# A fused attention and MLP kernel: work of the first batch moved between VectorE, ScalarE and GpSimd, score units reordered, last stores in two tiles

## Chip, cores, metric

One core of one Trainium2 chip (trn2). The metric is the device time of one execution in microseconds (us); less is better. Two kernels count as different when their executions differ by over 2%.

## The reference

Causal attention with a decay that is the cumulative sum of the positive part of `s`, in 8 batches of 8 heads, 576 positions and head size 64; then an MLP with exact gelu on the 4608 x 512 result.

```python
def _attn_ref(q, k, v, s):
    scores = scale * np.matmul(q, k.transpose(0, 1, 3, 2))
    cum = np.cumsum(np.maximum(s, 0.0), axis=-1)
    bias = -(cum[:, :, :, None] - cum[:, :, None, :])
    scores = np.where(causal, -1000000000.0, scores + np.minimum(bias, 0.0))
    attn = np.exp(scores - np.max(scores, axis=-1, keepdims=True))
    attn = attn / (np.sum(attn, axis=-1, keepdims=True) + 1e-09)
    return np.matmul(attn, v)

def _moe_ref(x, w_in, w_out):      # x: 4608 x 512, w_in: 512 x 2048, w_out: 2048 x 512
    h = x @ w_in
    return (0.5 * h * (1.0 + erf(h / sqrt(2)))) @ w_out
```

## The kernel before

The bias of key j is folded into v: row j of v is scaled by a weight `wb` and the weight itself is a 65th column, so one value matmul gives numerator and denominator. The parts that the change touches, with cuts marked:

```python
    def scale_v(b, st):
        n_st = 128 if st < ST - 1 else SL
        w = wb[:n_st, st, b * H : (b + 1) * H]
        nc.vector.tensor_tensor(
            vv[b % 2][:n_st, st, :, 0:D],
            raws[b, "v"][:n_st, st, :, :],
            w.unsqueeze(2).to_broadcast([n_st, H, D]),
            op=MULT,
        )

    def den_col(b):
        nc.vector.tensor_copy(vv[b % 2][:, :, :, D], wb[:, :, b * H : (b + 1) * H])
    # ...
    def av_item(b, g, it, later=False):      # value matmuls of four heads, one block of 128 queries
        # ... PE: lhsT=P[:, h, off:off+128], rhs=vv[b % 2][:, jt, 4*g+h, :]  (64 columns of v and the weight)
        nc.vector.reciprocal(rc[:n], o_ps[:n, :, D])
        nc.vector.tensor_tensor(x_of[b, it][...], o_ps[:n, :, 0:D], rc..., op=MULT)
    # ...
    # sc_first(g, u, halves, fill): score matmuls of group g, unit u, half by half, `fill` fillers, exp on ScalarE
    # mk_item: causal mask on P by VectorE;  to_xT: transposes on PE, copy to xT by VectorE
    # filler(n): n matmuls of zeros that keep PE busy
```

The eviction of the second layer, the order of the start, and the tail (the two copies of the tail are named in words here):

```python
            for sub in subs:
                o_sb = ost.tile([128, KO * 128], fp32, tag="osb", bufs=3, name="o_sb")
                if c == 0 and sub != 1:
                    nc.scalar.activation(o_sb, y_of[c, sub], func=AF.Copy)
                else:
                    nc.vector.tensor_copy(o_sb, y_of[c, sub])
                # ...
    load_v(0, nc.gpsimd, (0, 1))
    load_w(0, 0)
    load_w(0, 1)
    load_v(0, nc.gpsimd, (2, 3))
    load_w(0, 2)
    load_w(0, 3)
    # ... more loads, all issued by GpSimd, at most eight outstanding
    tr_qk(0, 0, 0)
    tr_qk(0, 1, 0)
    sc_first(0, 0)
    tr_qk(0, 0, 1)
    den_col(0)
    tr_qk(0, 1, 1)
    sc_first(0, 1, (0,))
    filler(2)
    sc_first(1, 0, (0,))
    mk_item(0, 0, 0)
    scale_v(0, 0)
    scale_v(0, 1)
    sc_first(1, 0, (1,))
    av_item(0, 0, 0)
    filler(1)
    mk_item(0, 1, 0, 0, 2)
    av_item(0, 0, 1)
    mk_item(0, 1, 0, 2, 4)
    sc_first(0, 1, (1,))
    filler(1)
    av_item(0, 1, 0)
    av_item(0, 1, 1)
    sc_first(1, 1, (0,), 0)
    to_xT(0, 0, True)
    filler(1)
    to_xT(0, 1, True)
    # ...
            o_sb = ost.tile([128, KO * 128], fp32, tag="osb", bufs=3, name="o_sb")
            for i, (copy, eng) in enumerate([(VectorE copy, nc.sync), (ScalarE copy, nc.scalar)]):
                cols = slice(i * 256, i * 256 + 256)
                copy(o_sb[:, cols], y[:, cols])
                eng.dma_start(out=out[r0 : r0 + 128, cols], in_=o_sb[:, cols])
```

## Time and profile before

| | before |
|---|---|
| median of 3 runs, us | 316.27 (315.94 to 316.29) |
| profiled run: time, span, us | 315.04, 313.3 |
| PE busy, granted clock | 96%, 0.998 |
| first score matmul, MLP start, us | 9.10, 18.52 |
| second layer of chunk 0, first layer of chunk 1 start, us | 35.81, 55.85 |
| last full eviction, last half copies (VectorE, ScalarE) start, us | 305.04, 308.96, 309.42 |

The profile is of one execution. PE is TensorE's matmuls (PEq its sequencer), DVE is VectorE, ACT is ScalarE, POOL is GpSimd and SP is SyncE; SBUF and PSUM are the on-chip memories, PSUM the one that matmuls write to. The granted clock is the share of TensorE's full clock that it was given. A landing is the end of a transfer. A timeline row has start, duration, engine, source line, operation, output and inputs, shape, the number of instructions merged in it, and in brackets the idle time of that engine just before with what ended it. Waits of a GpSimd load are for one of eight slots: load n waits for the landing of load n - 8.

### The profile page before, as it was taken

Reading aid. Unit: us, or ns where it says so; the run is one execution under the profiler, and the core shown is the slowest. Engines: PE = TensorE matmul, PEld = TensorE weight load, DVE = VectorE, ACT = ScalarE, POOL = GpSimd, SP = SyncE. Lnnn points to the kernel's source line nnn. Section 1 sums busy time; section 2 is a strip of 40 time slices with the busy share of each in tenths; the row PEclk is TensorE's granted clock in tenths of the full one; section 3 lists DMA queues with packets and bytes.
Section 4 is the critical chain, followed back from the end, with each engine's and each line's share of the span. In section 5 each row is a group of like instructions: output and inputs, shape, how many; then the busy total and the mean of one; then the engine's idle time right before and its main releaser. Section 6 shows DMA issues by size and latency. Waiting matters only on the chain. (4 is left out here: it accounts for less than half of the span.)

```text
span 313.3 us, 6063 instructions
## 1 busy us (share of the span) xinstructions
PE 301.7 (96%) x2478; PEld 155.6 (50%) x2520; DVE 200.0 (64%) x401; ACT 190.0 (61%) x256; POOL 53.0 (17%) x72
## 2 busy tenths in 40 slices
PE   8999999999999999999999999999999999999993
PEld 3487755544554455445454445444544555444441
DVE  7876657699769856975598559945895632250020
ACT  3686968877747673875586648756776666105400
POOL 8543440142002500070007000500000000000000
PEclk9999999999999999999999999999999999999999
DMA  7999999779521973188307961633101311010012
GB/s 135 219 229 211 225 216 284 149 144 209 143 74 27 210 168 96 25 172 199 103 18 173 175 137 32 145 74 96 52 17 42 103 52 25 33 68 36 1 68 75
DMA packets 30979, 36.46 MB, mean 116 GB/s; under 512 B 15648, under 2 KB 20000, under 8 KB 30944
## 3 DMA queue, kind: packets, MB, share of 16 engines
q0 software_dynamic: 11552, 23.07, 38.2%
q1 hardware_dynamic: 19248, 12.80, 14.2%
q8 instruction: 21, 0.34, 0.4%
q14 instruction: 14, 0.11, 0.1%
q10 hardware_dynamic: 144, 0.13, 0.1%
HBM read 36.85 MB, written 9.44 MB: 148 GB/s over the span
## 5 line engine op out<-in xcount | busy, mean ns | idle before, releaser
L483 PE MATMUL o_ps<-w_out_r,gT 128*128 128x512 bf16 x551 | 132.2, 379 | 2.4 <-issue 1.6
L467 PE MATMUL h_ps<-xT,w_in_r 128*128 128x512 bf16 (+1 forms) x625 | 131.4, 357 | 0.8
L472 ACT ACTIVATE gT<-h_ps 128x1024 bf16<-128x1024 f32 (+1 forms) x80 | 74.8, 939 | 63.6 <-PE h_ps L467 62.8
L467 PEld LDWEIGHTS <-w_in_r 128*128 128x128 bf16 x640 | 59.6, 98 | 53.8 <-issue 0.4
L483 PEld LDWEIGHTS <-gT 128*128 128x128 bf16 x576 | 51.9, 98 | 56.6 <-issue 3.1
L359 ACT ACTIVATE P<-sc_ps 128x1024 bf16<-128x1024 f32 x56 | 54.3, 1021 | 30.9 <-PE sc_ps L344 30.9
L122 POOL DMA_DIRECT2D raw_v<-in_v_dram x40 | 34.0, 864 | 128.0 <-ACT sq L213 115.9
L493 DVE COPY o_sb<-o_ps 128x512 f32<-128x512 f32 x32 | 22.1, 691 | 46.5 <-PE o_ps L483 46.5
L444 DVE RECIPROCAL rc<-av 128x4 f32<-128x4 f32 (+1 forms) x80 | 14.0, 175 | 39.4 <-PE av L435 39.4
L187 DVE STREAM_TRANSPOSE qkT<-raw_qk 128x576 f32<-128x576 f32 x32 | 37.4, 1243 | 0.7 <-DMA raw_qk<-in_k_dram 0.5
L435 PEld LDWEIGHTS <-P 128*128 128x128 bf16 x576 | 27.4, 98 | 17.2 <-DVE P L367 1.0
L445 DVE TENSOR_TENSOR x<-av,rc 128x256 bf16<-128x256 f32 (+1 forms) x80 | 33.8, 423 | 3.0
L205 DVE TENSOR_REDUCE amx<-raw_qk 128x2 f32<-128x2304 bf16 x14 | 35.1, 2534 | 0.0
L435 PE MATMUL av<-vv,P 128*128 128x65 bf16 x576 | 30.5, 193 | 1.0 <-DVE P L367 0.3
L221 DVE TENSOR_TENSOR vv<-raw_v,wb 128x512 bf16<-128x512 f32 (+1 forms) x40 | 26.0, 690 | 3.0 <-DMA raw_v<-in_v_dram 3.0
L367 DVE TENSOR_TENSOR P<-P,tri_bf 128x1024 bf16<-128x1024 bf16 (+1 forms) x33 | 22.1, 669 | 8.7 <-ACT P L359 8.7
L213 ACT ACTIVATE sq<-raw_v 128x512 bf16<-128x512 f32 (+1 forms) x40 | 24.9, 622 | 0.0
L344 PE MATMUL sc_ps<-qkT 32*128 32x256 bf16 (+2 forms) x560 | 18.2, 250 | 0.0
L344 PEld LDWEIGHTS <-qkT 32*128 32x128 bf16 x560 | 11.7, 92 | 12.4 <-issue 11.6
L498 ACT ACT_TABLE_LOAD x8 | 10.3, 1283 | 0.9 <-PEq L819 0.7
L419 PE MATMUL f_ps<-zero 128*128 128x512 bf16 x29 | 9.4, 448 | 1.2 <-DVE zero L150 1.2
L501 ACT ACT_TABLE_LOAD x8 | 10.3, 1283 | 0.1
(79 smaller groups left out, 89.9 us busy)
## 6 DMA issues: line engine op xcount, KB each, us to landing
out_dram<-o_sb SPq DMA_DIRECT2D x35, 256.0 KB, 2.2
raw_v<-in_v_dram POOLq DMA_DIRECT2D x32, 256.0 KB, 5.8
raw_qk<-in_q_dram POOLq DMA_DIRECT2D x7, 576.0 KB, 7.9
raw_qk<-in_k_dram POOLq DMA_DIRECT2D x7, 576.0 KB, 10.3
w_in_r<-in_moe_w_in_dram POOLq DMA_DIRECT2D x4, 512.0 KB, 11.8
w_out_r<-in_moe_w_out_dram POOLq DMA_DIRECT2D x4, 512.0 KB, 16.3
raw_v<-in_v_dram POOLq DMA_DIRECT2D x8, 128.0 KB, 6.6
raw_qk<-in_q_dram POOLq DMA_DIRECT2D x2, 288.0 KB, 5.5
```

The lines of the kernel that those rows point to most:

```text
L122: eng.dma_start(out=t[:n_st, st, :, :], in_=bass.AP(tensor=v.tensor, offset=v.offset + b * H * S * D + st * 128 * D, ap=[[D, n_st], [S * D ...
L187: nc.vector.transpose(qkT[b % 2][:, i, g, :S, :].rearrange("p s e -> p (s e)").bitcast(fp32) .rearrange("p (l j) -> p j l", j=LT), raws[b, ...
L205: nc.vector.tensor_reduce(amx[:, b * HG + g], raws[b, "qk"][:, :, g, :], axis=AX, op=ALU.max, apply_absolute_value=True,)
L213: nc.scalar.activation(sq[:n_st], raws[b, "v"][:n_st, st].rearrange("p h d -> p (h d)"), func=AF.Square, accum_out=sumv[:n_st, b, st : st ...
L221: nc.vector.tensor_tensor(vv[b % 2][:n_st, st, :, 0:D], raws[b, "v"][:n_st, st, :, :], w.unsqueeze(2).to_broadcast([n_st, H, D]), op=MULT,)
L344: nc.tensor.matmul(s_ps[h // 2][:, h % 2, off : off + n], lhsT=qk[r, 1, g, jt * 128 : jt * 128 + 128, e], rhs=qk[r, 0, g, i0 : i0 + n, e], ...
L359: nc.scalar.activation(P[:, 2 * h2 : 2 * h2 + 2, o : o + 512], s_ps[h2], func=AF.Exp, scale=scale)
L435: nc.tensor.matmul(o_ps[:, h, :], lhsT=P[:, h, off : off + 128], rhs=vv[b % 2][:, jt, 4 * g + h, :], start=(i == 0), stop=(i == len(BLK[it ...
L445: nc.vector.tensor_tensor(x_of[b, it][:n, g * 256 : g * 256 + 256].rearrange("p (h d) -> p h d", d=D), o_ps[:n, :, 0:D], rc[:n].unsqueeze( ...
L467: nc.tensor.matmul(h_ps[:, i, :], lhsT=w_in_r[:, ko, ft * 128 : (ft + 1) * 128], rhs=xT[:, ko, c * NB + n0 : c * NB + n1], start=(ko == 0) ...
L472: nc.scalar.activation(gT_of[c][:, f2 * 2 : f2 * 2 + 2, n0:n1], h_ps, func=AF.Gelu)
L483: nc.tensor.matmul(y_of[c, sub], lhsT=gT[:, ft, sub * 128 : (sub + 1) * 128], rhs=w_out_r[:, ft, :], start=(ft == 0), stop=(ft == FT - 1),)
```

## The change

The intent is to take VectorE off the path to the MLP: the denominators' column goes to ScalarE, the scaling of v's second block to GpSimd, the value matmuls of group 0 go ahead of a late score unit and four fillers go. The eviction of subtile 1 of chunk 0 goes to ScalarE. In the tail each half gets its own tile.

```diff
@@ -215,10 +215,10 @@
             accum_out=sumv[:n_st, b, st : st + 1],
         )
 
-    def scale_v(b, st):
+    def scale_v(b, st, eng=nc.vector):
         n_st = 128 if st < ST - 1 else SL
         w = wb[:n_st, st, b * H : (b + 1) * H]
-        nc.vector.tensor_tensor(
+        eng.tensor_tensor(
             vv[b % 2][:n_st, st, :, 0:D],
             raws[b, "v"][:n_st, st, :, :],
             w.unsqueeze(2).to_broadcast([n_st, H, D]),
@@ -487,7 +487,7 @@
         if f1 == FT and store:
             for sub in subs:
                 o_sb = ost.tile([128, KO * 128], fp32, tag="osb", bufs=3, name="o_sb")
-                if c == 0 and sub != 1:
+                if c == 0:
                     nc.scalar.activation(o_sb, y_of[c, sub], func=AF.Copy)
                 else:
                     nc.vector.tensor_copy(o_sb, y_of[c, sub])
@@ -514,6 +514,7 @@
     cum_sum()
     masks()
     weights()
+    nc.scalar.activation(vv[0][:, :, :, D], wb[:, :, 0:H], func=AF.Copy)
     filler(3)
     filler(3, raws[0, "qk"][:, 1, 0, :128])
     load_v(0, nc.gpsimd, (0, 1))
@@ -522,6 +523,7 @@
     load_v(0, nc.gpsimd, (2, 3))
     load_w(0, 2)
     load_w(0, 3)
+    scale_v(0, 1, nc.gpsimd)
     load_v(0, nc.gpsimd, (4,))
     load_qks(1)
     load_w(1, 0)
@@ -534,29 +536,25 @@
     tr_qk(0, 1, 0)
     sc_first(0, 0)
     tr_qk(0, 0, 1)
-    den_col(0)
     tr_qk(0, 1, 1)
     sc_first(0, 1, (0,))
-    filler(2)
+    filler(1)
     sc_first(1, 0, (0,))
     mk_item(0, 0, 0)
     scale_v(0, 0)
-    scale_v(0, 1)
-    sc_first(1, 0, (1,))
+    sc_first(1, 0, (1,), 0)
     av_item(0, 0, 0)
-    filler(1)
+    av_item(0, 0, 1)
     mk_item(0, 1, 0, 0, 2)
-    av_item(0, 0, 1)
+    sc_first(0, 1, (1,))
     mk_item(0, 1, 0, 2, 4)
-    sc_first(0, 1, (1,))
-    filler(1)
+    sc_first(1, 1, (0,), 0)
     av_item(0, 1, 0)
     av_item(0, 1, 1)
-    sc_first(1, 1, (0,), 0)
+    sc_first(1, 1, (1,), 0)
     to_xT(0, 0, True)
     filler(1)
     to_xT(0, 1, True)
-    sc_first(1, 1, (1,), 0)
     mk_item(0, 0, 1)
     scale_v(0, 2)
     mk_item(0, 1, 1)
@@ -794,14 +792,14 @@
     with tc.manual_schedule():
         for sub in range(LAST[1], 4):
             y = y_of[LAST[0], sub]
-            o_sb = ost.tile([128, KO * 128], fp32, tag="osb", bufs=3, name="o_sb")
             r0 = LAST[0] * NB + sub * 128
             for i, (copy, eng) in enumerate(
                 [(nc.vector.tensor_copy, nc.sync), (lambda o, a: nc.scalar.activation(o, a, func=AF.Copy), nc.scalar)]
             ):
                 cols = slice(i * 256, i * 256 + 256)
-                copy(o_sb[:, cols], y[:, cols])
-                eng.dma_start(out=out[r0 : r0 + 128, cols], in_=o_sb[:, cols])
+                o_sb = ost.tile([128, KO * 128], fp32, tag="osb", bufs=3, name="o_sb")[:, :256]
+                copy(o_sb, y[:, cols])
+                eng.dma_start(out=out[r0 : r0 + 128, cols], in_=o_sb)
 
 
 # ---- launch: one core; inputs and outputs as the reference has them ----
```

## The prediction

> **What bounds the kernel now.** I read the page from the top, then the start (first 60 us) and the last 18 us as timelines engine by engine, then the landing times of single transfers.
>
> The page's busy shares and slices:
>
> ```profile
> PE 301.7 (96%) x2478; PEld 155.6 (50%) x2520; DVE 200.0 (64%) x401; ACT 190.0 (61%) x256; POOL 53.0 (17%) x72
> PE   8999999999999999999999999999999999999993
> PEclk9999999999999999999999999999999999999999
> DMA  7999999779521973188307961633101311010012
> ```
>
> PE is busy from the first slice to the last at full clock; DMA is near full only in the first quarter. A gain must therefore remove PE waiting, or shorten the tail after the last matmul. The change touches three places: 9 to 20 us, 47 to 49 us, and the tail.
>
> The timelines of PE and DVE at the start (start, duration, engine, line, operation, idle time before and its releaser):
>
> ```profile
> 13.06 0.63 PE L389 MATMUL sc_ps<-qkT 32*128 32x256 bf16 x8
> 13.85 0.29 PE L435 MATMUL av<-vv,P 128*128 128x65 bf16 x4
> 14.19 0.40 PE L435 MATMUL av<-vv,P 128*128 128x65 bf16 x8
> 16.09 0.48 PE L435 MATMUL av<-vv,P 128*128 128x65 bf16 x10 [0.33 <-DVE P L367]
> 18.52 3.65 PE L467 MATMUL h_ps<-xT,w_in_r 128*128 128x256 bf16 x32
> ...
> 10.73 1.26 DVE L187 STREAM_TRANSPOSE qkT<-raw_qk 128x576 f32<-128x576 f32 x1
> 12.43 1.26 DVE L221 TENSOR_TENSOR vv<-raw_v,wb 128x512 bf16<-128x512 f32 x2
> 14.17 0.18 DVE L444 RECIPROCAL rc<-av 128x4 f32<-128x4 f32 x1 [0.48 <-PE av L435]
> 15.62 0.41 DVE L367 TENSOR_TENSOR P<-P,tri_bf 128x512 bf16<-128x512 bf16 x1
> 17.50 0.97 DVE L413 COPY xT<-xt_ps 128x512 bf16<-128x512 bf16 x2
> ```
>
> The MLP starts at 18.52 because the second xT copy ends at 18.47. Back from there the chain is DVE: reciprocal and scaling of each value item, the two half masks, the value matmuls at 16.09 that waited for the second mask. PE's fillers (0.21 us each) lie in its shadow.
>
> The second batch's stage, PE then DVE, and the tail's chain:
>
> ```profile
> 48.40 0.40 PE L435 MATMUL av<-vv,P 128*128 128x65 bf16 x8 [0.30 <-DVE xT L413]
> 47.33 0.68 DVE L493 COPY o_sb<-o_ps 128x512 f32<-128x512 f32 x1
> 47.93 0.75 DVE L413 COPY xT<-xt_ps 128x512 bf16<-128x512 bf16 x2
> 45.94 0.60 ACT L491 ACTIVATE o_sb<-o_ps 128x512 f32<-128x512 f32 x1 [0.66 <-PE o_ps L483]
> 46.95 1.94 ACT L359 ACTIVATE P<-sc_ps 128x1024 bf16<-128x1024 f32 x2 [0.42 <-PE sc_ps L344]
> ...
> 308.96 0.44 DVE o_sb L803
> 309.40 0.02 issue
> 309.42 0.38 ACT o_sb L800
> ```
>
> PE waited at 48.40 for an xT copy that stood behind the eviction at 47.33. In the tail ScalarE copies its half only after VectorE's, since both write one tile.
>
> **What the Trainium skill says.** "GPSIMD Engine Reference", Performance versus the Vector engine, puts a GpSimd tensor_tensor at about 2.6 cycles an element at 1.2 GHz (4497 ns for 2048 fp32). My estimate for 512 elements is 512 x 2.6 / 1.2 = 1.11 us plus some 0.1 us of dispatch, so 1.2 us against the 0.69 us on VectorE. The trace of before has no such instruction; its two affine selects of 128 elements start 0.25 us apart, 1.95 ns an element with one input, which fits. "SBUF — State Buffer", Who interferes with whom, says a VectorE instruction with two SBUF inputs contends with a GpSimd instruction that reads SBUF; no run yet shows it. VectorE's remaining scaling would hold the port until about 13.12. "DMA: Bandwidth & Descriptors", Issuing engines are not separate DMA queues, says that SP and ACT share the same 16 DMA engines; the tail agrees: two 128 KB stores, and the engines 90 to 99% busy at 310.8 to 311.1. "TensorE: Matmul & The Clock Gate", Part 1, says an idle window of about 3.4 us halves the clock. The trace grants full clock throughout with the fillers in; without four of them no gap I foresee exceeds 0.7 us.
>
> **The change part by part.**
>
> *Denominators on ScalarE.* Removes a 0.34 us copy at 10.35 from VectorE; ScalarE has 1.90 us idle before its first exponential at 9.76. But the transpose behind the removed copy started at 10.73, just when the last k block landed (issued 3.00, 7.7 us to landing, so 10.7). Worth 0.0.
>
> *One scaling on GpSimd.* It stands behind a weight load (10.99 to 11.74) and needs v's second block: issued at about 5.0, 7.9 us to landing, so 12.9. With the port free at 13.12 it starts at about 13.15, ends at 13.15 + 1.2 = 14.35, and PE sees it at T = 14.4. The next loads on this queue are issued some 2 us later (12.15 becomes 14.4), but eight transfers are outstanding and the DMA engines stay full, so landings should not move.
>
> *Reordering.* The first value item may start at 13.64, without its filler, and finish its VectorE part by 14.6. The second starts at T = 14.4, against 14.19 before. VectorE then does reciprocal (T + 0.43 = 14.83), scaling (+0.22), half mask (+0.34 = 15.39), half mask (+0.33 = 15.72, ends 16.13): before, that last mask ended at 16.03. So 0.1 us later. PE does the late score units meanwhile; the one between xT blocks is now ahead of them. From the mask on the chain is as before (16.03 to 18.52 is 2.49 us), so the MLP starts at 16.13 + 2.49 = 18.62, +0.1 us. Break-even is T = 14.3. The four fillers removed (4 x 0.21 = 0.85 us) are worth nothing directly. The last exponential would end near 18.4 instead of 19.63, but PE next needs a gelu only at 22.50, when the first is over by 21.6: worth 0.
>
> A gain here would also be cut short by the DMA. Two landings (issue times from the GpSimd timeline, then times to landing of those two issues, third quarter-blocks of weights):
>
> ```profile
> 10.99 0.75 POOL L147 DMA_DIRECT2D w_in_r<-in_moe_w_in_dram x1 [0.71 <-DMA raw_qk<-in_k_dram]
> DMA to landing us min/median/max: 13.9/13.9/13.9
> 25.17 1.51 POOL L147 DMA_DIRECT2D w_out_r<-in_moe_w_out_dram x2 [1.91 <-DMA w_in_r<-in_moe_w_in_dram]
> DMA to landing us min/median/max: 15.3/15.3/15.3
> ```
>
> The last block of the first weight lands at 10.99 + 13.9 = 24.9, and PE uses it at 24.95; the third of the second weight lands at 40.5 and is used at 40.59. So PE runs on the heels of its weights, and at most 0.1 us of an earlier MLP start survives. A later start is not recovered. I take +0.1 us for the stage.
>
> *Eviction of subtile 1 on ScalarE.* VectorE loses 0.68 us at 47.33, so the xT copy starts at 47.33 and ends at 47.75, and PE's value item goes at 47.94 instead of 48.40. ScalarE evicts at about 46.45 to 47.0, where it waited 0.42 us anyway. The next value item (49.50) needs a scaling that ended at 49.28 and would end at about 49.16, so only 49.50 - 49.22 = 0.28 us survives. PE is the bound from there to the end with no other wait for data, so it stays: -0.28 us.
>
> *Two tiles for the last halves.* ScalarE's copy moves from 309.42 to 308.96 and its store from 309.84 to about 309.38: 0.46 us. But data flow without a break from 310.25 to 311.19, 0.94 us for 262 KB (280 GB/s). Started together, at the 340 GB/s of the best tenths they take 0.77 us: end at 311.02, so -0.17 us instead of -0.46.
>
> Sum: +0.1 - 0.28 - 0.17 = -0.35 us, and 316.27 - 0.35 = 315.9 us.
>
> **The rivals.** (1) GpSimd is fast or starts early (T at 14.0): the chain gains 0.3 us, but the weights' landing lets only 0.1 us through: about 315.7. (2) GpSimd becomes the bound: its first elementwise instruction of this kind may carry a start-up cost, or the port is lost to VectorE. Each 0.5 us beyond T = 14.4 goes straight into the time; 316.4 to 317. For it: spans on this engine are the ones I know least; against: the queue is otherwise only issuing. (3) PE cools down for lack of fillers: half clock for some 3 us costs 1.5 us or more, about 317.5. Against: the gaps stay short and PE was dense before. (4) The weights land later because loads are issued 2 us later: against it, only transfers behind the fourth w_in block move, and the DMA is full; it would cost up to 0.5 us. (5) The tail gains its full 0.46 us because two queues overlap better: 315.6.
>
> **Range and chances.** Centre 315.9. The gain side is capped near 0.1 + 0.46 + 0.46 = 1.0 us (315.2); the loss side is rival 2 or 4, some 0.6 us (316.6). Times of before spread by 0.35 us, which the range covers too: 315.2 to 316.6. Two per cent is 6.3 us, more than any part can move: within 2% 0.98, faster 0.01, slower 0.01.
>
> **What would show it.** Right: no den copy on VectorE at 10.35 and the transpose still at 10.7; a GpSimd multiply of about 1.2 us from about 13.15; PE's second value item at about 14.4 waiting for GpSimd; MLP start at 18.5 to 18.8; PE's wait of 0.30 us for the xT copy gone; both tail copies at the same time, but last data only 0.1 to 0.3 us earlier. Wrong: a GpSimd span over 1.7 us or an MLP start beyond 19; a granted clock below 9 tenths in the first slices; PE waiting for w_in or w_out near 25 or 40 us; a total that moves by more than 1 us.

## The result

| | before | changed |
|---|---|---|
| median of 6 runs, us | 315.86 (315.35 to 316.29) | 315.62 (315.31 to 316.13) |
| ratio | | 0.9993, 95% interval 0.9979 to 1.0007 |
| profiled run, us | 315.04 | 315.94 |

The ratio is the mean time of one kernel's runs over that of the other's of the same rounds, so it is not quite the ratio of the medians. 315.62 lies in the predicted range. The gain is smaller than the spread of the runs, so single times say little here. I compare stages inside the traces, each counted from its own beginning.

The start of the changed kernel: PE, VectorE, ScalarE and GpSimd timelines.

```profile
10.23 0.63 PE L389 MATMUL sc_ps<-qkT 32*128 32x256 bf16 x8 [0.47 <-DVE qkT L187]
14.64 0.33 PE L435 MATMUL av<-vv,P 128*128 128x65 bf16 x5
15.21 0.37 PE L435 MATMUL av<-vv,P 128*128 128x65 bf16 x7 [0.24 <-POOL vv L221]
19.46 3.65 PE L467 MATMUL h_ps<-xT,w_in_r 128*128 128x256 bf16 x32 [0.52 <-DVE xT L413]
...
11.88 1.26 DVE L187 STREAM_TRANSPOSE qkT<-raw_qk 128x576 f32<-128x576 f32 x1 [0.27 <-DMA raw_qk<-in_k_dram]
13.58 0.67 DVE L221 TENSOR_TENSOR vv<-raw_v,wb 128x512 bf16<-128x512 f32 x1
14.98 0.18 DVE L444 RECIPROCAL rc<-av 128x4 f32<-128x4 f32 x1 [0.73 <-PE av L435]
...
8.53 0.38 ACT L517 ACTIVATE vv<-wb 128x40 bf16<-128x40 bf16 x1
14.05 1.10 POOL L221 TENSOR_TENSOR vv<-raw_v,wb 128x512 bf16<-128x512 f32 x1 [1.17 <-DMA raw_v<-in_v_dram]
```

Everything stands about 1.1 us later than before because the loads came later in this execution: the fourth transpose starts at 11.88 against 10.73, on its landing both times. That differs from execution to execution (the table of all traces below): the block was issued at 3.00 us before and 3.01 us here, and landed 7.7 and 8.8 us later. In all traces this took 7.2 to 8.8 us with a scaling on GpSimd and 7.0 to 8.0 us without, so a part of it may be the change's own; that is not shown. From the first score to the MLP it is 19.46 - 10.23 = 9.23 us against 18.52 - 9.10 = 9.42, a gain of 0.19 us where I had forecast a loss of 0.1. PE waited 0.24 us for GpSimd, and VectorE stood idle 0.73 us where it used to do the second scaling.

The second batch's stage and the tail of the changed kernel (timelines, then the chain that ended last: start, duration, engine):

```profile
48.65 0.39 PE L410 MATMUL xt_ps<-ident_bf,x 128*128 128x128 bf16 x4
48.88 0.41 PE L435 MATMUL av<-vv,P 128*128 128x65 bf16 x8
48.27 0.42 DVE L413 COPY xT<-xt_ps 128x512 bf16<-128x512 bf16 x1
46.87 1.09 ACT L491 ACTIVATE o_sb<-o_ps 128x512 f32<-128x512 f32 x2 [0.65 <-PE o_ps L483]
...
309.48 0.44 DVE o_sb L801
309.91 0.02 issue
309.94 0.38 ACT o_sb L797
```

PE's value item now follows the transposes without a wait, and from the second layer to the second chunk it is 56.48 - 36.74 = 19.74 us against 20.04. In the tail nothing changed: ScalarE's copy still starts 0.46 us after VectorE's, when that is done.

### The profile page after: what moved, and what is told of

It is laid out like the page before. It is cut to its first block, busy times and chain, and to the rows that moved or that the text cites. A ratio compares the mean times of both kernels' runs of the same rounds, so it can differ in the third digit from the quotient of the medians.

```text
span 314.2 us, 6059 instructions
## 1 busy us (share of the span) xinstructions
PE 302.0 (96%) x2475; PEld 155.5 (49%) x2516; DVE 199.0 (63%) x398; ACT 191.0 (61%) x258; POOL 54.5 (17%) x73
## 3 DMA queue, kind: packets, MB, share of 16 engines
q1 hardware_dynamic: 19248, 12.80, 14.4%
## 5 line engine op out<-in xcount | busy, mean ns | idle before, releaser
L493 DVE COPY o_sb<-o_ps 128x512 f32<-128x512 f32 x31 | 21.4, 691 | 46.5 <-PE o_ps L483 46.5
```

## The experiments

Twelve runs were made, of nine new kernels and, once more, the changed one. The stages of all traces, in us:

| run | first score | first score to MLP | first layer | second layer, to chunk 1 | last full eviction to last copy | span |
|---|---|---|---|---|---|---|
| before | 9.10 | 9.42 | 17.29 | 20.04 | 3.92 | 313.3 |
| changed | 10.23 | 9.23 | 17.28 | 19.74 | 3.93 | 314.2 |
| s_vec | 9.42 | 9.03 | 18.04 | 19.75 | 3.88 | 313.7 |
| s_twice | 9.01 | 12.10 | 18.06 | 19.73 | 4.18 | 316.4 |
| s_den | 9.87 | 9.20 | 18.66 | 19.73 | 4.02 | 315.3 |
| s_fill | 9.43 | 9.67 | 17.29 | 19.72 | 5.11 | 315.2 |
| t_banks | 9.88 | 9.21 | 17.41 | 19.73 | 5.97 | 316.7 |
| t_banks_one | 9.17 | 9.13 | 17.66 | 19.73 | 5.94 | 316.3 |
| e_only | 9.00 | 9.43 | 17.66 | 19.94 | 5.19 | 315.1 |
| w_early | 8.68 | 8.98 | 18.12 | 19.79 | 3.76 | 313.0 |
| after5 | 10.08 | 9.21 | 17.29 | 19.72 | 3.90 | 313.9 |
| vec5 | 8.73 | 9.09 | 18.37 | 19.73 | 3.77 | 313.3 |
| e_only3 | 9.54 | 9.42 | 17.28 | 19.72 | 4.16 | 314.6 |
| w_early2 | 9.12 | 8.99 | 17.29 | 20.63 | 4.00 | 313.6 |

### s_vec: the second scaling back on VectorE, in the new order

```diff
-    scale_v(0, 1, nc.gpsimd)
...
     scale_v(0, 0)
+    scale_v(0, 1)
```

> The changed kernel with the second scaling of v put back on VectorE, right after the first, everything else as changed. Measure: from the start of the fourth transpose of q and k (it starts when the last k block has landed, so the run's own loading speed drops out) to the first MLP matmul; 7.79 us in the profile of before (10.73 to 18.52), 7.58 us in that of the changed kernel (11.88 to 19.46). Theory: the gain of 0.21 us comes from the new order alone. VectorE stood idle 0.73 us before the first reciprocal, and a scaling of 0.69 us (0.6 us from start to start) fits there; its result would be ready some 0.3 us before GpSimd's. So 7.45 to 7.6 us. Rival: GpSimd's taking over the scaling is what pays; then VectorE's chain gets 0.6 us longer and this run shows 8.0 to 8.2 us.

It was 18.45 - 11.01 = 7.44 us from the fourth transpose to the MLP, a hair under the theory's range and far from the rival's. VectorE's and PE's timelines:

```profile
12.71 1.41 DVE L221 TENSOR_TENSOR vv<-raw_v,wb 128x512 bf16<-128x512 f32 x2
14.10 0.18 DVE L444 RECIPROCAL rc<-av 128x4 f32<-128x4 f32 x1
18.45 3.65 PE L467 MATMUL h_ps<-xT,w_in_r 128*128 128x256 bf16 x32 [0.52 <-DVE xT L413]
22.89 1.05 PE L467 MATMUL h_ps<-xT,w_in_r 128*128 128x256 bf16 x8 [0.31 <-DMA w_in_r<-in_moe_w_in_dram]
```

Both scalings fit before the first reciprocal, which no longer waits. So the gain is there without GpSimd, which takes 0.14 to 0.2 us of it back. It need not be the order's alone: this kernel also has the four fillers fewer, and s_fill below shows that they count. The old order without these fillers was not run. The last row shows the second finding: PE, early, waits for the first weight, and the first layer takes 18.04 us in place of 17.28.

### s_twice: GpSimd scales twice

```diff
     scale_v(0, 1, nc.gpsimd)
+    scale_v(0, 1, nc.gpsimd)
```

> The changed kernel with GpSimd doing its scaling twice (same result, the second over the first). Theory: the scaling on GpSimd lies on the chain to the MLP, since PE waited for it by 0.24 us and VectorE's chain follows; so the doubled 1.10 us goes straight into the measure: 7.58 + 1.0 to 1.1 = 8.6 to 8.7 us. Rival: it lies beside VectorE's and ScalarE's work with slack; then less than 0.5 us shows (under 8.1 us).

It was 21.11 - 10.43 = 10.68 us, 3.1 us more and not 1.05. GpSimd's row, PE's wait for it, and what the stretches were granted (columns: stretch, length, then busy time of PE, its weight loads, VectorE, ScalarE and GpSimd, each with its number of instructions, PE's granted clock, DMA share, GB/s):

```profile
12.80 2.17 POOL L221 TENSOR_TENSOR vv<-raw_v,wb 128x512 bf16<-128x512 f32 x2 [1.35 <-DMA raw_v<-in_v_dram]
15.02 0.37 PE L435 MATMUL av<-vv,P 128*128 128x65 bf16 x7 [1.38 <-POOL vv L221]
...
13.30:15.00 1.70, 0.34 (x7) 0.24 (x6) 0.60 (x2) 1.18 (x2) 1.62 (x3) 1.00 1.24 205
15.00:17.00 2.00, 1.51 (x27) 1.26 (x29) 1.27 (x4) 1.01 (x1) 2.00 (x3) 0.73 1.21 271
17.00:19.00 2.00, 2.00 (x34) 1.65 (x28) 1.10 (x4) 1.04 (x2) 0.86 (x2) 0.50 1.12 215
21.00:23.00 2.00, 1.89 (x11) 1.35 (x11) 2.00 (x6) 0.61 (x2) 0.70 (x2) 0.57 1.25 218
```

The wait grew by 1.38 - 0.24 = 1.14 us, which is the second scaling: GpSimd's result is on the path. Most of the rest, some 2 us, goes with the clock: after that wait PE was granted half of it from about 16 to 22 us, and from its second value item to the MLP it took 21.11 - 15.02 = 6.09 us against 19.46 - 15.21 = 4.25. The first layer began at this clock too. That is my rival of the cooling, met here and not in the changed kernel, whose wait was short. It was seen in this one execution; a wait of 1.10 us in s_den left the clock at 1.00.

### s_den: the denominators' column back on VectorE

```diff
-    nc.scalar.activation(vv[0][:, :, :, D], wb[:, :, 0:H], func=AF.Copy)
...
     tr_qk(0, 0, 1)
+    den_col(0)
     tr_qk(0, 1, 1)
```

> The changed kernel with the denominators' column back on VectorE, between the third and the fourth transpose. Theory: the fourth transpose waits for the landing of the last k block anyway, so the 0.34 us copy costs nothing: the measure stays at 7.58 us (7.5 to 7.65), and first transpose of the block to MLP likewise unless the block lands early. Rival: the copy delays the fourth transpose; then the transpose follows the copy without a wait for a transfer and the third-transpose-to-MLP time (9.11 us in the changed kernel, 10.35 to 19.46) grows by 0.3 us.

```profile
11.09 0.34 DVE L229 COPY vv<-wb 128x40 bf16<-128x40 bf16 x1
11.48 1.25 DVE L187 STREAM_TRANSPOSE qkT<-raw_qk 128x576 f32<-128x576 f32 x1
11.74 0.75 POOL L147 DMA_DIRECT2D w_in_r<-in_moe_w_in_dram x1 [0.73 <-DMA raw_qk<-in_k_dram]
24.32 1.05 PE L467 MATMUL h_ps<-xT,w_in_r 128*128 128x256 bf16 x8 [1.10 <-DMA w_in_r<-in_moe_w_in_dram]
```

From the fourth transpose to the MLP 19.07 - 11.48 = 7.59 us, and 9.20 us from the first score (9.23 with the column on ScalarE): the copy costs nothing. The transpose starts when the k block has landed: GpSimd's load, which waits for the same landing, follows 0.26 us later here as in before (10.73 and 10.99) and as in the changed kernel, which has no copy there (11.88 and 12.14). The third transpose to the MLP was 9.08 us (9.11), so the rival falls. In this run the weights were later still, and PE waited 1.10 us for them.

### s_fill: the four fillers put back

```diff
     sc_first(0, 1, (0,))
-    filler(1)
+    filler(2)
...
-    sc_first(1, 0, (1,), 0)
+    sc_first(1, 0, (1,))
     av_item(0, 0, 0)
+    filler(1)
     av_item(0, 0, 1)
...
     mk_item(0, 1, 0, 2, 4)
+    filler(1)
     sc_first(1, 1, (0,), 0)
```

> The changed kernel with its four removed fillers put back (one behind the first late score unit, one in the second of them, one between the two value items, one ahead of the next score unit). My prediction called them worth nothing directly. Theory: they lie partly in the shadow of VectorE's chain; at most the one ahead of the first value item delays a reciprocal, so 7.6 to 7.85 us. Rival 1: PE is the bound here and all four count, 4 x 0.21 = 0.85 us: 8.4 us. Rival 2: without them PE cools; then this run shows a higher granted clock at the start than the changed kernel, whose slices all show 9 tenths or more.

The measure that I had named reads 19.10 - 10.21 = 8.89 us, above theory and rival, and does not serve: in this run the k block landed early and VectorE then stood idle 0.61 us for ScalarE's exponential, so the chain did not hang on the fourth transpose. From the first score it is 9.67 us against 9.23: 0.44 us more, half of what all four fillers take (0.85 us), between theory and rival, and 0.25 us more than before: with these fillers kept, the changed start gains nothing. The granted clock was the same, so no cooling without them. One row besides was not foreseen. GpSimd and VectorE:

```profile
12.58 1.09 POOL L221 TENSOR_TENSOR vv<-raw_v,wb 128x512 bf16<-128x512 f32 x1 [1.36 <-DMA raw_v<-in_v_dram]
12.69 1.53 DVE L221 TENSOR_TENSOR vv<-raw_v,wb 128x512 bf16<-128x512 f32 x1
```

Here GpSimd's scaling started first, and VectorE's own took 1.53 us in place of 0.67, ending 0.55 us after GpSimd's end. It ended at 14.22 and the first value matmul ran at 14.27. By PE's own pace it would have come at about 14.17 (the filler before it at 13.95, and from a filler to a value matmul 0.22 us from start to start, 14.39 to 14.61 in this trace). So my estimate is that the blocked scaling has about 0.1 us of the 0.44 and the fillers the rest.

### t_banks and t_banks_one: the last subtile's sums in two banks of PSUM

The core of the edit, and with one output tile again in the second kernel:

```diff
+        if (c, subs[0]) == LAST:
+            for i in range(2):
+                y = yps.tile([128, 256], fp32, tag="mlp", bufs=2, name="o_ps")
+                for ft in range(FT):   # 256 columns of w_out each
+                    nc.tensor.matmul(y, lhsT=gT[...], rhs=w_out_r[:, ft, i * 256 : i * 256 + 256], ...)
...
-                copy(o_sb, y[:, cols])
+                copy(o_sb, y[i])
```

> The changed kernel with the last subtile's sums in two banks of PSUM, 256 columns each (16 + 16 matmuls of 256 columns in place of 16 of 512), so that VectorE and ScalarE each read a bank of their own; the two output tiles stay. In the changed kernel ScalarE's copy still waited for VectorE's (309.48 then 309.94), as before (308.96 then 309.42), so the two tiles took away no wait. Theory: what ScalarE waits for is the shared PSUM bank. Then both copies start within 0.05 us here, ScalarE's store is issued some 0.4 us sooner after VectorE's copy starts, and the last data of the stores end 0.1 to 0.25 us sooner, measured from the start of VectorE's copy (2.2 us in the profile of before). Rival: ScalarE comes late out of the branch for another reason; then it still starts 0.46 us behind.

> As the run with two banks, but with one output tile for both halves, as in the kernel before. Theory: the tile in SBUF never made the wait (the halves are disjoint columns), so both copies start within 0.05 us here too. Rival: the tile makes a wait of its own; then ScalarE starts 0.4 to 0.46 us behind VectorE even with two banks, and it took both changes.

The tail of the run with two banks and two tiles, then with two banks and one tile:

```profile
311.29 0.38 ACT L815 ACTIVATE o_sb<-o_ps 128x256 f32<-128x256 f32 x1 [15.30 <-PEq L676]
311.29 0.42 DVE L819 COPY o_sb<-o_ps 128x256 f32<-128x256 f32 x1 [5.28 <-PEq L676]
```

```profile
310.88 0.38 ACT L816 ACTIVATE o_sb<-o_ps 128x256 f32<-128x256 f32 x1 [15.29 <-PEq L676]
310.88 0.42 DVE L819 COPY o_sb<-o_ps 128x256 f32<-128x256 f32 x1 [5.26 <-PEq L676]
```

Both copies start at the same instant, with two tiles and with one. What made ScalarE wait lay in PSUM; the tile in SBUF had no part in it. The edit gives each half a bank and also a PSUM tile of its own; two tiles in one bank were not run, so bank and PSUM tile are not told apart. The Trainium skill, "PSUM — Partial Sum Buffer", section "PSUM bank collisions raise a hardware error", says that two engines may not read one bank of the same partitions at once and that software has to order them. The traces agree: 0.46 us of order with one bank, none with two.

The bulk of the stores' data ended 2.1 us after VectorE's copy began (2.2 before, 2.3 in the changed kernel), about what I had worked out. Yet the stores landed 3.1 and 3.3 us after their issue, in both runs, against 1.9 and 1.8 before (1.8 to 2.4 in all twelve other traces), and the execution ended 5.4 us after the copy began (4.3 before, 4.7 changed). And the copies themselves began 5.97 and 5.94 us after the last full eviction in place of 3.93, released by PE's sequencer at the branch. So in these two executions the copies start about 2 us later: 318.53 and 318.03 us in the profiled runs. These 5.97 us are not the branch alone, since the last subtile's matmuls lie in them: from their end, as the profile models it, to the copies it is 0.51 us before (308.45 to 308.96) and 2.51 us in t_banks (308.78 to 311.29). Why the branch is later was not tested, and the two banks need not be the reason. One thing goes with it: the four traces with over 5 us in that column of the table (s_fill, t_banks, t_banks_one, e_only) are the four whose queue q8 of instruction transfers shows 22 packets; the ten others show 21.

### e_only and e_only3: the kernel before with the one eviction on ScalarE

```diff
-                if c == 0 and sub != 1:
+                if c == 0:
```

> The kernel before with nothing but the eviction of subtile 1 of the first chunk moved to ScalarE. Measure: from the first matmul of the first chunk's second layer to the first matmul of the second chunk; 20.04 us before, 19.72 to 19.75 us in the changed kernel and in the four runs so far. Theory: this part alone makes those 0.3 us: 19.70 to 19.78 us, with the wait of PE for the xT copy gone; the start (first score to MLP) stays at 9.4 us. Rival: the shift of the start makes the difference; then 20.0 us here.

The first run read 19.94 us, between theory and rival, because PE waited for the second weight in it:

```profile
41.36 1.89 PE L483 MATMUL o_ps<-w_out_r,gT 128*128 128x512 bf16 x8 [0.41 <-DMA w_out_r<-in_moe_w_out_dram]
48.43 0.41 PE L435 MATMUL av<-vv,P 128*128 128x65 bf16 x8
...
310.39 0.42 DVE L803 COPY o_sb<-o_ps 128x256 f32<-128x256 f32 x1 [4.50 <-PEq L666]
```

> The kernel before with the one eviction on ScalarE, again, three rounds. In its first run the stage gained (19.94 against 20.04 us, though with a wait of 0.4 us for w_out in it), but the last copy came 1.2 us later after the branch than in before, released by PE's sequencer, with a third instruction fetch in the last 12 us where before has two; so had the run with the fillers put back. Theory: that late branch belongs to the program as laid out (same in every execution); then this kernel is 0.8 to 1.0 us slower than before in all rounds and its trace shows it again. Rival: it is chance; then it is 0.2 to 0.4 us faster than before and the trace most likely shows 3.9 us from the last full eviction to the last copy. The stage without a wait for w_out is to show 19.70 to 19.78 us.

The same kernel again, with no such wait:

```profile
48.15 0.39 PE L410 MATMUL xt_ps<-ident_bf,x 128*128 128x128 bf16 x4
48.37 0.41 PE L435 MATMUL av<-vv,P 128*128 128x65 bf16 x8
...
309.72 0.42 DVE L803 COPY o_sb<-o_ps 128x256 f32<-128x256 f32 x1 [3.47 <-PEq L666]
```

The stage took 19.72 us, with the start at 9.42 us: this part alone makes the 0.3 us. The late branch of the first run (5.19 us from the last full eviction to the last copy) was 4.16 us in the second, so the size of it is not fixed by the program; it varies from execution to execution. Its four times were 315.42 to 316.64 us, ratio 0.999 (0.996 to 1.0019): "always slower by 0.8 us" falls, and the gain is too small to be timed.

### w_early and w_early2: the first weight loaded ahead of v's later blocks (wrong results on purpose)

```diff
-    load_v(0, nc.gpsimd, (2, 3))
     load_w(0, 2)
     load_w(0, 3)
-    scale_v(0, 1, nc.gpsimd)
+    load_v(0, nc.gpsimd, (2, 3))
     load_v(0, nc.gpsimd, (4,))
...  (in scale_v, blocks 2 and 3 of batch 0 read raw blocks 0 and 1)
     scale_v(0, 0)
+    scale_v(0, 1)
```

> Wrong results on purpose: the changed kernel with both scalings on VectorE, whose third and fourth blocks of v are taken from the first two, so that their loads can go behind the four blocks of the first weight; these then have 512 KB less ahead of them (some 2.5 us at 205 GB/s). The kernel with both scalings on VectorE reached the MLP 0.2 us sooner than the changed one (9.03 against 9.23 us from the first score), but then PE waited 0.3 us and more for the weight and the first layer took 18.04 us instead of 17.28. Theory: the weights' landing eats the gain of the start; with the weights early the first layer takes 17.25 to 17.35 us with no wait for the weight, and the start stays at 9.0 to 9.1 us. Rival: the new order makes the first layer slower by itself; then it takes 17.7 us or more here too.

The first layer took 18.12 us, against the theory, but with no wait for the weight: what it waited for was the fifth block of v (1.0 us), whose load I had moved back. So in the second kernel `load_v(0, nc.gpsimd, (4,))` stands ahead of `load_v(0, nc.gpsimd, (2, 3))`:

> Wrong results on purpose, as the run with early weights, with the fifth block of v ahead of the third and fourth: in the first such run no wait for w_in was left, but PE waited 1.0 us for the fifth block's scaling (0.2 us otherwise), because its load had been put last; the first layer took 18.12 us. Theory: with that load early too the first layer takes 17.25 to 17.4 us, no wait for w_in, start 8.95 to 9.1 us, so the whole gain of the start arrives at the second layer. Rival: the new order slows the first layer by itself; 17.7 us or more.

The first layer took 17.29 us with the start at 8.99: the order does not slow it, the weight's landing does. PE's waits in that trace up to 58 us (who waited for what, us, times, longest):

```profile
PE o_ps L483 <- DMA w_out_r<-in_moe_w_out_dram: 1.1, 1, 1.1
PE h_ps L467 <- DVE xT L413: 0.5, 1, 0.5
```

So the gain reached the second layer at 35.40 us, and was lost there to the second weight (20.63 us in place of 19.73). Only in part because PE came sooner: this block of the weight landed at 24.92 + 16.4 = 41.3 us, against 40.5 in before. The second chunk began at 56.03 us, no sooner than in runs with a slow start (55.85 before).

### after5 and vec5: the changed kernel and the version without GpSimd's scaling, five rounds

> The changed kernel again, five rounds, for a trace of its own and beside the same rounds of the kernel before. From the parts measured so far (start -0.2, eviction -0.3, tail 0) 0.2 to 0.6 us under before, so a ratio of 0.998 to 0.9995. Theory on the weights: wherever the start got ahead of the loads, PE waits for w_in between 22 and 26 us, so the gain of the start is lost in some executions. Start 9.2 to 9.25 us from the first score, second layer to second chunk 19.72 to 19.75 us, ScalarE's last copy 0.46 us behind VectorE's.

> The version without GpSimd's scaling (both on VectorE, order and eviction as changed), five rounds: the candidate that should beat both. Theory: 0.2 us less than the changed kernel up to the MLP (9.0 to 9.05 us against 9.23), all or part of which the landing of w_in takes back: so 0 to 0.2 us under the changed kernel and 0.3 to 0.7 us under before. Rival: GpSimd's relief of VectorE pays later; then it is slower than the changed kernel by 0.2 us or more.

| | before | after5 | vec5 |
|---|---|---|---|
| median, us | 316.16 (11 runs) | 315.65 (6 runs) | 315.24 (6 runs) |
| lowest to highest | 315.35 to 317.1 | 315.24 to 318.06 | 314.87 to 315.62 |
| ratio, 95% | | 1.0001 (0.9969 to 1.0033) | 0.997 (0.9949 to 0.9991) |

The changed kernel's stages repeat to 0.02 us (9.21, 17.29, 19.72). Its ratio missed the range that I had expected (0.998 to 0.9995) and does not resolve a gain; nor did PE wait for a weight in its trace. The version without GpSimd (the program of s_vec) has the lowest median and is the only one whose interval lies under 1: 0.3% under before. Its start is shorter by 0.12 us here, which the wait for the first weight (0.6 us) would swallow. What else differs between it and the changed kernel, which is one instruction apart, is in GpSimd's first rows, here of s_vec and then of the changed kernel:

```profile
3.86 0.34 POOL L156 TENSOR_SCALAR_AFFINE_SELECT uptri<-uptri 128x128 f32<-128x128 f32 x1
4.10 1.86 POOL L122 DMA_DIRECT2D raw_v<-in_v_dram  x2
```

```profile
3.88 0.60 POOL L156 TENSOR_SCALAR_AFFINE_SELECT uptri<-uptri 128x128 f32<-128x128 f32 x1
4.43 1.83 POOL L122 DMA_DIRECT2D raw_v<-in_v_dram  x2
```

An instruction that stands far ahead of the scaling takes 0.26 us longer, and the loads of v and of the weights are issued 0.33 us later. This is so in every trace: first load of v at 4.43 or 4.44 us in the seven with a scaling on GpSimd, at 4.10 or 4.11 in the seven without (before, s_vec, e_only, w_early, vec5, e_only3, w_early2). VectorE's first transpose is likewise at 6.29 or 6.30 against 6.07 or 6.08. Loads issued 0.33 us later would fit the 0.4 us between the medians of vec5 and after5, which is also their distance at the second chunk (55.92 and 56.30 us). But PE waits for no weight in after5's trace, so that link is not shown. That the scaling brings the delay is shown by these pairs; how an instruction that comes later does so is not.

## Why the prediction was right, and where not

The range held, but that says little: it is 1.4 us wide, and the interval of the ratio, 0.9979 to 1.0007, holds no change as well as a gain of over 0.6 us. That the sum (-0.35 us forecast, -0.24 us between the medians of 6) came near is luck, since two terms were off in opposite directions.

- **Denominators on ScalarE, worth 0.0**: right. s_den has the transpose start at the landing with the copy in front of it.
- **One scaling on GpSimd, T = 14.4**: mis-sized. Counted from the fourth transpose I had 14.4 - 10.73 = 3.67 us to PE's second value item; it was 15.21 - 11.88 = 3.33. I had GpSimd wait for VectorE's scaling to end and then take 1.2 us. Its record starts before that end (14.05 against 13.58 + 0.67 = 14.25), yet the wait seems real: in all six traces where VectorE goes first, GpSimd's (first) scaling ends 0.89 to 0.92 us after VectorE's, whether its record began 0.12 us before that end (1.04 us long, s_den) or 0.37 us (1.26 us long, t_banks_one). So what was too large is the 1.2 us after the wait: 0.9 us. My own break-even of 3.57 us then gives -0.24 us, and the traces show -0.19 and -0.21 in place of +0.1. That GpSimd is on the path was right (s_twice), and so was that it is slower than VectorE would have been (s_vec). Missing altogether is the 0.33 us by which it makes all loads of v and weights later; my argument that later loads would not matter was about those behind the scaling only.
- **The fillers, worth nothing directly**: wrong, by 0.44 us with the blocked scaling in it and, by my estimate, 0.34 us without (s_fill). In the new order PE reaches the first value item by its own pace, and fillers in front of it count; they do not all lie in VectorE's shadow.
- **A gain of the start cut short by the weights' landing, at most 0.1 us let through**: not so in the changed kernel's two traces, where PE waited for no weight and the first layer took 17.28 and 17.29 us (17.29 before). It can happen, though, and then costs more than I wrote: the landing moves from execution to execution, and in s_vec, s_den and vec5 PE waited 0.3, 1.1 and 0.6 us. w_early2 shows the gain pass the first weight and be taken at the second, whose landing was later too.
- **Eviction on ScalarE, -0.28 us**: right. 20.04 to 19.74 and 19.72, and alone 19.72 (e_only3).
- **Two tiles for the last halves, -0.17 us**: the step that failed. I took the wait as one for the tile ("since both write one tile"); t_banks_one shows that this tile makes none, and t_banks that the shared bank (or tile) of PSUM does. The term measured 0. Its second half, that two stores started together end only 0.17 us sooner, was near for the data's bulk (2.1 against 2.2 us) but the landing came later.
- **PE cooling**: no sign in the changed kernel. It was seen once, after a wait of 1.38 us (s_twice), and not after one of 1.10 us (s_den).

What stays open: the shares of the order and of the fillers in the gain of the start, whether bank or PSUM tile makes the tail's wait, the cause of the late branch in some executions, and how the scaling on GpSimd delays that engine's first loads.

## What to carry to other kernels

A wait that is released by another engine's instruction names the engine, not the resource: before splitting a tile, ask what else the two instructions share, a bank of PSUM first. Before moving work to an idle engine, compare when each engine would deliver: here GpSimd delivered later and VectorE stood idle for 0.73 us. Look also at what the receiving engine does besides (here it issues the loads). And where a start is fed by transfers that land just before they are used, the next landing can take a faster chain's gain back, as in s_vec and vec5, so look at the landings of all later inputs first.

## What the Trainium skill lacked or had wrong

- "TensorE: Matmul & The Clock Gate", Part 1, names an idle window of about 3.4 us for the drop to half clock. In s_twice a granted clock of 0.50 from about 16 to 22 us followed a wait of 1.38 us, and in the 3.4 us before the drop (12.55 to 15.95) PE was busy 2.02 us. So PE need not be idle for the whole window; how idle is not shown.
- "SBUF — State Buffer", Who interferes with whom, has the later of two such instructions blocked. With GpSimd first, VectorE's scaling took 1.53 us in place of 0.67, which agrees. With VectorE first (six traces), GpSimd's record starts 0.12 to 0.37 us before VectorE's end and ends 0.89 to 0.92 us after it, which agrees too. The page does not say that the record of a blocked GpSimd instruction can start before the block ends.
- "GPSIMD Engine Reference", Performance versus the Vector engine, times tensor_tensor with fp32 inputs only. With a 32-bit and a broadcast 16-bit input 512 elements took 1.04 to 1.10 us in six traces (1.26 us in t_banks_one, blocked longest), two in a row 2.17 us: the 2.6 cycles an element (1.11 us, an estimate from the page) hold.
- "DMA: Bandwidth & Descriptors", Issuing engines are not separate DMA queues, says that issuing from two engines saves only issue time. It does not say what they do to each other's landing. In t_banks and t_banks_one, two 128 KB stores issued 0.03 and 0.04 us apart landed 3.1 and 3.3 us after issue; in the twelve other traces, issued 0.18 to 0.42 us apart, after 1.8 to 2.4 us. That the nearness is the cause is not shown.
- No page read here tells of a GpSimd instruction that slows earlier ones: with one elementwise multiply in its program, GpSimd's second affine select took 0.59 to 0.60 us in place of 0.33 to 0.34 and its first load of v was issued 0.33 us later, in 7 of 7 traces against 0 of 7.
